# Mixer weights by rows, without a copy at the start, and a shorter last chunk: what each part is worth in a recurrent attention and mixer kernel

## The chip, the cores and the metric

One core of one Trainium2 chip. The metric is device time in microseconds (us) of one execution of the whole program; lower is better. Absolute times differ between chips by up to 16 us for the same kernel, so kernels are compared by their ratio to the kernel before, run on the same chip in the same rounds.

## The reference

Two layers, each an attention over 64 segments of 32 tokens with 8 memory tokens that pass from segment to segment, and a mixer MLP whose four quarters of `h` are shifted by one or two tokens. Cut to what matters:

```python
# x: (1, 2048, 640); 32 heads of 192; w1, w2 640x640; w3 640x1536; w4 1536x640
def _A_ref(x, mem0, Wq, Wk, Wv, Wo, seg_len):
    mem = mem0
    for s in range(n_seg):                       # 64 segments, one after another
        h = concat([mem, x[segment s]])          # 40 tokens
        q, k, v = h @ Wq, h @ Wk, h @ Wv
        o = softmax(mask(q k^T * scale)) v @ Wo
        mem = o[:, :8];  outs.append(o[:, 8:])

def _B_ref(x, w1, w2, w3, w4):
    h = gelu(layernorm(x) @ w1)                  # 640
    g0..g3 = the quarters of h, shifted by +1, -1, +2, -2 tokens
    x1 = x + concat([g0, g1, g2, g3]) @ w2
    return x1 + gelu(layernorm(x1) @ w3) @ w4

x = x + A(layernorm(x));  x = x + B(layernorm(x))     # layer 1
x = x + A(layernorm(x));  x = x + B(layernorm(x))     # layer 2, same weights
```

## The kernel before

The kernel runs the two layers side by side, layer 2 five segments behind layer 1: 69 attention steps, and beside them 35 mixer chunks of 128 columns (two layers of 64 tokens). Chunk c runs beside steps 2c+2 and 2c+3; chunk 33 runs beside the last step, 68, and chunk 34 alone behind it. In layer 1 chunk 34 has nothing, in layer 2 the last 34 tokens.

A planner puts every instruction in order. Each is given a time at which it is due, in units of `STEP` = 48 us. Weights that are not resident pass through a ring of 16 tiles of 128x768. Attention and mixer share the ring; the largest share of each is a constant, and the loads of a share that is full wait in the plan. Attention weights are loaded by the SP queue, mixer weights by GpSimd.

```python
RING = 16          # weight tiles in the ring
RING_A = 14        # at most for attention
RING_B = 6         # at most for the mixer
STEP = 48.0
W3 = (0.7, 0.04)   # w3's n-th product is due at base + STEP * (0.7 + 0.04 n)
W4 = (1.5, 0.025)
W2 = (0.4, 0.04)
...
def load_b(c, nm, n, due):                       # one mixer weight tile
    b = ring("rb")
    k = {"w1": n, "w3": KC + n, "w2": KC + FC - 4 + n}.get(nm)
    if nm == "w4":
        src, rd = w4_v[:, n, :], []
    elif nm == "w2" and n < 4:
        src, rd = B_w2[QD * n:QD * n + P, :], []
    else:
        src, rd = wbd[k], [B("wbd", k)]          # from scratch memory
    ...                                          # nc.gpsimd.dma_start(out=..., in_=src)

def order_mixer_weights():                       # at the start, DRAM to DRAM
    for n in range(KC):                          # w1: column blocks made contiguous
        ... nc.gpsimd.dma_start(out=o, in_=w1[:, :, QD * n:QD * n + P])
    ...                                          # a part of w2, and w3 (12 copies)
    for n in range(FC):
        ... nc.gpsimd.dma_start(out=o, in_=B_w3.rearrange("(kc p) n -> p kc n", p=P)[:, :, P * n:P * n + P])
...
# chunk(c): w1, three output blocks in a PSUM bank, one weight tile per output block
for n in range(a, e):
    wb, wv = load_b(c, "w1", n, due)
    for kc in range(KC):
        nc.tensor.matmul(out=o[:, n - a, :], lhsT=w[:, kc * P:(kc + 1) * P],
                         rhs=vT[:, kc, 4:XB + 4], start=(kc == 0), stop=(kc == KC - 1))
...
# chunk_end(c): w4
for n in range(FC):
    wb, wv = load_b(c, "w4", n, due)             # y2 += h2T[n]^T w4[n], 2 matmuls of 320
...
# the order is final; at most 10 transfers of the SP queue are in flight
for o in placed:
    ins = o.fn(o)
    if o.dma and o.e == "SP":
        if len(flight) >= FLIGHT:                # FLIGHT = 10
            ...                                  # waits for flight[-FLIGHT]
```

## Time and profile before

| | before |
|---|---|
| median of 3 runs | 3567.71 us (3561.39 to 3569.81) |
| span of the profiled run | 3573.5 us |
| first attention step ends | 106.5 us |
| from there to the end of step 67 | 3364.0 us |
| step 68 and chunk 33, to chunk 33's last product | 55.7 us |
| chunk 34 alone, to the end | 47.3 us |

The last four rows are the stages. They come from the view of busy time in chosen stretches. Its columns are start:end, length, then busy us and count of PE (TensorE), PEld (weight loads), DVE, ACT, POOL (GpSimd), then the granted TensorE clock, the DMA engines' busy share, GB/s. For the kernel before:

```profile
0.00:106.50 106.50, 59.43 (x1172) 48.28 (x1172) 21.35 (x91) 19.93 (x49) 29.34 (x55) 1.00 1.00 345
106.50:3470.50 3364.00, 3270.87 (x82106) 3156.11 (x82104) 2308.03 (x6825) 1660.21 (x3466) 875.51 (x1577) 0.99 0.94 309
3470.50:3526.20 55.70, 50.22 (x1297) 43.54 (x1294) 34.85 (x122) 23.11 (x56) 22.19 (x42) 1.00 0.94 310
3526.20:3573.50 47.30, 18.39 (x145) 12.60 (x141) 19.94 (x49) 7.20 (x15) 21.18 (x38) 0.65 0.34 110
```

The reader is to see three limits: transfers in the first row (share 1.00), TensorE in the second and third (3270.87 of 3364.00), and a chain of latencies in the last (TensorE busy 18 of 47 us, DMA share 0.34).

### The profile page before, as it was taken

The page shows a single profiled execution, that of the slowest core. Times are in us where ns is not written, and L with a number is a line of the kernel's source. Part 1 is how long each engine was busy: PE and PEld are TensorE (multiplying, and loading weights), DVE is VectorE, ACT ScalarE, POOL GpSimd, SP SyncE. Part 2 cuts the span into 40 slices and gives each one's busy share as a digit, 9 for nine tenths or more (in the row PEclk, how much of TensorE's full clock was granted, in tenths as well). Part 3 has the DMA queues.
Part 4 walks back from the last instruction along what each step waited for, and adds up shares of the span by engine and source line. Part 5 has one row for each costly group of instructions (what it writes and reads, how often), then busy time and mean ns, then how long its engine had stood idle before and what let it go on. Part 6 is the DMA issues. An engine that isn't in the chain of part 4 may idle for free.

```text
span 3573.5 us, 194593 instructions
## 1 busy us (share of the span) xinstructions
PE 3398.9 (95%) x84703; PEld 3260.5 (91%) x84703; DVE 2384.2 (67%) x7085; ACT 1710.5 (48%) x3584; POOL 948.2 (27%) x1712
## 2 busy tenths in 40 slices
PE   5899999999999999999999999999999999999996
PEld 4788999999999999999999999999999999999885
DVE  2456667777676777776666777776767777776555
ACT  2344555554454555544455555454545555444432
POOL 3022222222222222222222222222222222222224
PEclk9999999999999999999999999999999999999898
DMA  9999999999999999999999999999999999999996
GB/s 342 310 314 312 305 302 304 310 308 308 309 307 313 314 308 304 316 300 308 306 308 311 311 301 305 308 319 308 309 311 310 311 306 313 309 304 316 310 313 207
DMA packets 735993, 1097.76 MB, mean 307 GB/s; under 512 B 97374, under 2 KB 693612, under 8 KB 735136
## 3 DMA queue, kind: packets, MB, share of 16 engines
q1 hardware_dynamic: 669504, 874.19, 74.6%
q0 software_dynamic: 65632, 211.12, 17.9%
q8 instruction: 662, 10.85, 1.3%
q14 instruction: 195, 1.60, 0.1%
HBM read 1079.68 MB, written 8.19 MB: 304 GB/s over the span
## 4 chain that ended last, share of the span: by engine, by line
PE 69%; DMA 19%; issue 9%; POOL 2%; DVE 1%; ACT 0%; POOLq 0%; SPq 0%; ACTq 0%; DVEq 0%
PE psy L669 14%; PE psq L530 12%; PE psv L571 11%; PE psk L530 11%; DMA wst<-in_A_Wk_dram 7%; DMA wst<-in_A_Wq_dram 5%; PE psvt L583 4%; DMA wst<-in_B_w_dram 4%; PE pss L602 3%; PE pso L650 3%; PE psh L993 3%; DMA wst<-in_A_Wv_dram 3%; PE pst L635 2%; PE y L1011 2%; POOL wst L465 1%
## 5 line engine op out<-in xcount | busy, mean ns | idle before, releaser
L530 PEld LDWEIGHTS <-wst 128*128 128x128 bf16 x13248 | 551.9, 100 | 75.1 <-DMA wst<-in_A_Wk_dram 41.3
L587 ACT COPY V<-psvt 80x768 bf16<-80x768 bf16 (+1 forms) x552 | 438.2, 794 | 327.7 <-PE psvt L583 326.2
L465 POOL DMA_DIRECT2D wst<-in_B_w_dram x560 | 303.6, 542 | 1005.2 <-PE psk L530 250.6
L656 DVE CAST oT<-pso 128x480 bf16<-128x480 f32 (+1 forms) x552 | 340.8, 617 | 341.7 <-PE pso L650 341.0
L465 POOL DMA_DIRECT2D wst<-wbd x630 | 339.6, 539 | 724.8 <-PE pss L602 229.5
L669 PE MATMUL psy<-oT,wo 128*128 128x80 bf16 (+1 forms) x10350 | 509.6, 199 | 11.2 <-DMA wo<-in_A_Wo_dram 5.1
L538 ACT CAST qT<-psq 128x480 bf16<-128x480 f32 (+1 forms) x552 | 292.3, 530 | 428.8 <-PE psq L530 427.5
L530 PE MATMUL psk<-hT,wk 128*128 128x80 bf16 (+1 forms) x9936 | 482.7, 199 | 7.9 <-ACT hT L707 4.2
L571 PE MATMUL psv<-hT,wv 128*128 128x80 bf16 (+1 forms) x9936 | 466.6, 199 | 6.5 <-DMA wv<-in_A_Wv_dram 4.3
L530 PE MATMUL psq<-hT,wq 128*128 128x80 bf16 (+1 forms) x9936 | 454.5, 199 | 9.8 <-DMA wq<-in_A_Wq_dram 8.7
L577 ACT CAST vTs<-psv 128x480 bf16<-128x480 f32 (+1 forms) x552 | 292.3, 529 | 337.2 <-PE psv L571 335.5
L669 PEld LDWEIGHTS <-wo 128*128 128x128 bf16 x10350 | 425.6, 100 | 21.3 <-issue 9.2
L530 PEld LDWEIGHTS <-wk 128*128 128x128 bf16 x9936 | 411.6, 99 | 21.9 <-issue 8.8
L571 PEld LDWEIGHTS <-wv 128*128 128x128 bf16 x9936 | 399.8, 100 | 18.7 <-DMA wv<-in_A_Wv_dram 5.7
L613 DVE CUSTOM_DVE_ANT_1 pss<-pss,mask 80x320 f32<-80x320 f32 (+1 forms) x512 | 245.4, 479 | 253.8 <-PE pss L602 252.3
L530 PEld LDWEIGHTS <-wq 128*128 128x128 bf16 x9936 | 395.5, 100 | 16.3 <-DMA wq<-in_A_Wq_dram 9.5
L530 PE MATMUL psk<-hT,wst 128*128 128x80 bf16 (+1 forms) x6624 | 359.0, 199 | 32.2 <-DMA wst<-in_A_Wk_dram 28.2
L571 PE MATMUL psv<-hT,wst 128*128 128x80 bf16 (+1 forms) x6624 | 368.0, 199 | 8.7 <-DMA wst<-in_A_Wv_dram 4.8
L625 DVE TENSOR_REDUCE sm<-pss 80x4 f32<-80x320 f32 (+1 forms) x552 | 252.7, 458 | 153.6 <-ACT pss L620 153.1
L669 PE MATMUL psy<-oT,wst 128*128 128x80 bf16 (+1 forms) x6210 | 353.0, 199 | 1.0 <-DMA wst<-in_A_Wo_dram 0.5
L530 PE MATMUL psq<-hT,wst 128*128 128x80 bf16 (+1 forms) x6624 | 333.2, 200 | 16.3 <-DMA wst<-in_A_Wq_dram 14.3
L546 DVE CAST kT<-psk 128x320 bf16<-128x320 f32 (+1 forms) x552 | 254.7, 461 | 136.9 <-PE psk L530 132.6
(119 smaller groups left out, 5768.8 us busy)
## 6 DMA issues: line engine op xcount, KB each, us to landing
wst<-in_A_Wk_dram SPq DMA_DIRECT2D x1104, 192.0 KB, 4.7
wst<-in_A_Wq_dram SPq DMA_DIRECT2D x1104, 192.0 KB, 4.9
wst<-in_A_Wv_dram SPq DMA_DIRECT2D x1104, 192.0 KB, 4.9
wst<-in_A_Wo_dram SPq DMA_DIRECT2D x1242, 160.0 KB, 4.4
wst<-wbd POOLq DMA_DIRECT2D x630, 160.0 KB, 5.1
wst<-in_B_w_dram POOLq DMA_DIRECT2D x560, 160.0 KB, 4.9
wk<-in_A_Wk_dram SPq DMA_DIRECT2D x8, 576.0 KB, 7.3
wq<-in_A_Wq_dram SPq DMA_DIRECT2D x8, 576.0 KB, 7.5
```

The source lines that it names most:

```text
L465: return (nc.sync if B_SP else nc.gpsimd).dma_start(out=T(b)[:, 0:Dm], in_=src)
L530: nc.tensor.matmul(out=o[:, c, 0:N], lhsT=w[:, c * P:(c + 1) * P], rhs=h[:, kc, c0:c0 + N], start=pq.begin(), stop=True, skip_group_check= ...
L538: nc.scalar.copy(out=q[:, :, 0:N], in_=T(pq)[:, :, 0:N])
L546: nc.vector.tensor_copy(out=k4[:, :, 0::3, 0:N], in_=p4[:, :, 0::2, 0:N])
L571: nc.tensor.matmul(out=o[:, c, 0:N], lhsT=w[:, c * P:(c + 1) * P], rhs=h[:, kc, c0:c0 + N], start=pv.begin(), stop=True, skip_group_check= ...
L577: nc.scalar.copy(out=vs[:, :, 0:N], in_=T(pv)[:, :, 0:N])
L583: nc.tensor.transpose(out=T(pt)[0:N, c, :], in_=vs[:, c, 0:N], identity=ident[:, :])
L587: nc.scalar.copy(out=V_[0:N, :, 0:Dh], in_=T(pt)[0:N].rearrange("n c f -> n (c f)").rearrange("n (i e) -> n i e", i=HG))
L613: nc.vector.tensor_tensor_reduce(out=o, in0=o, in1=maskt.unsqueeze(1).to_broadcast([N, HG, N]), scale=-scale, scalar=3.0e38, op0=ALU.add, ...
L625: nc.vector.reduce_sum(out=sm_[0:N, 4:4 + HG], in_=o, axis=AX.X)
L656: nc.vector.tensor_copy(out=o_[:, :, 0:N], in_=T(pso)[:, :, 0:N])
L669: nc.tensor.matmul(out=T(psy[j])[:, m - m0, c0:c0 + N], lhsT=w[:, m * P:(m + 1) * P], rhs=o_[:, c, 0:N], start=psy[j].begin(), stop=True, ...
```

## The change

The intent: w1 and w3 are read by rows straight from the inputs, so that no rearranged copy is needed; the loops over output blocks and over the inner dimension change places, and two PSUM banks stay open. The last chunk is cut to the 72 columns that it needs, and its input rows and all its weights are loaded early into attention weights that are done with. Chunk 33 is made due earlier. The mixer's share of the ring falls from 6 to 5 slots. Cut to its core:

```diff
-RING_B = 6
+RING_B = 5
-W3 = (0.7, 0.04)
+W3 = (0.75, 0.055)
+W1 = (0.15, 0.04)
 ...
 def load_b(c, nm, n, due):
+    if c == NCH - 1:
+        return ahead[nm, n]
     b = ring("rb")
-    (scratch memory or input)
+    wd, src = mixer_src(nm, n)      # rows of w1, w2, w4; half rows (128x768) of w3
 ...
-def order_mixer_weights(): ...      # 24 copies, 2.95 MB
 ...
+def prefetch(c):                    # the last chunk's 32 weight tiles, on the SP queue
+    for i, (nm, n) in enumerate(units):
+        b, tl = resident["kqv"[i // 3 % 3], i // 9]      # a freed attention weight
+        ... nc.sync.dma_start(out=tl[:, i % 3, 0:wd], in_=src)
 ...
 def chunk(c):
-    D = lambda x: base + x * STEP
+    D = lambda x: base + x * STEP * (0.6 if c == NCH - 2 else 1.0)
+    last = c == NCH - 1
+    xn = XL if last else XB         # 72 or 128 columns
+    if last:
+        prefetch(c)
 ...
-    w1: for n: (load tile n) for kc: matmul
+    pz = [ps("B", [P, 3, XB], f32, "psh") for _ in range(2)]
+    for kc in range(KC):
+        wb, wv = load_b(c, "w1", kc, due)
+        for n in range(KC):
+            nc.tensor.matmul(out=T(pz[n // 3])[:, n % 3, 0:xn], lhsT=w[:, P * n:P * n + P],
+                             rhs=vT[:, kc, 4:xn + 4], start=pz[n // 3].begin(), stop=True, ...)
 ...                                 # w3 likewise, in two halves of 5 tiles
 def chunk_loads(c):
+    if c == NCH - 1:                # rows into a freed tile, not into xo behind its store
+        ... nc.gpsimd.dma_start(out=xl_view()[1:2 * (S - w0):2, :], in_=x2d[w0:S, :])
```

## The prediction

> **What bounds the kernel now.** I read the page's head first, then the busy time in chosen stretches, then the waits of TensorE, then the timelines of the last 50 us. The first two views show three stages with different limits (columns of the stretches: start:end, length, then busy us and count of PE, PEld, DVE, ACT, POOL, then granted clock, DMA share, GB/s):
>
> ```profile
> span 3573.5 us, 194593 instructions
> PE 3398.9 (95%) x84703; PEld 3260.5 (91%) x84703; DVE 2384.2 (67%) x7085; ACT 1710.5 (48%) x3584; POOL 948.2 (27%) x1712
> ...
> 20.00:40.00 20.00, 9.27 (x167) 7.27 (x168) 2.62 (x10) 3.07 (x7) 9.99 (x17) 1.00 1.05 367
> 60.00:80.00 20.00, 14.84 (x295) 11.98 (x292) 5.17 (x22) 5.13 (x12) 0.00 (x0) 1.00 1.07 371
> ...
> 2000.00:3000.00 1000.00, 980.20 (x24359) 955.24 (x24356) 704.95 (x2033) 505.45 (x1033) 265.89 (x478) 1.00 0.95 309
> ...
> 3530.00:3550.00 20.00, 7.64 (x50) 5.39 (x51) 10.42 (x28) 2.68 (x6) 9.64 (x17) 0.50 0.27 84
> ```
>
> The start (to about 107 us, where the first attention step ends) is bound by transfers: 367 to 371 GB/s while TensorE is 46 to 74% busy. The middle is bound by TensorE with transfers close behind: 24,359 matmuls in 1000 us is 41 ns each, and TensorE idles only 20 us of 1000. An attention step takes about 50.5 us there (from the copies that pass the memory tokens on); what I can add up from start to start of its matmuls without gaps over 60 ns is about 48.6 us, so only some 1.8 us a step, 36 us of each 1000, is waiting. The waits say for what (waiter, what ended it, us in all, times, longest):
>
> ```profile
> PE psk L530 <- DMA wst<-in_A_Wk_dram: 28.2, 47, 1.6
> PE y L1011 <- DMA wst<-in_B_w_dram: 16.4, 30, 1.6
> PE psq L530 <- DMA wq<-in_A_Wq_dram: 8.7, 7, 3.5
> ...
> PEld L530 <- DMA wst<-in_A_Wk_dram: 41.3, 77, 1.7
> PEld L1011 <- issue: 22.3, 44, 1.8
> ```
>
> The end is a chain of latencies: TensorE 38% busy at clock 0.50. In the timelines (start, length, operation, and in brackets the idle time before it), the last attention product ends at 3520.35; then come chunk 33's last product and the whole of chunk 34:
>
> ```profile
> 3520.35 2.06 PE L1011 MATMUL y<-wst,h2T 128*128 128x320 bf16 x14
> 3524.02 2.18 PE L1011 MATMUL y<-wst,h2T 128*128 128x320 bf16 x10 [1.61 <-DMA wst<-in_B_w_dram]
> 3537.80 2.83 PE L939 MATMUL psh<-vT,wst 128*128 128x128 bf16 x25 [0.78 <-ACT vT L914]
> 3550.86 5.17 PE L993 MATMUL psh<-vT,wst 128*128 128x128 bf16 x60 [0.83 <-ACT vT L981]
> 3561.34 1.24 PE L1011 MATMUL y<-wst,h2T 128*128 128x320 bf16 x6 [0.85 <-DMA wst<-in_B_w_dram]
> ...
> 3529.52 0.62 POOL L815 MEMSET xo<- 128x640 bf16 x1
> 3530.43 0.58 POOL L823 DMA_DIRECT2D xo<-x2d  x1 [0.29 <-POOL xo L815]
> ...
> 3532.56 0.82 DVE L861 TENSOR_TENSOR xw<-psx,xo 128x640 f32<-128x640 bf16 x1 [2.23 <-DMA xo<-x2d]
> ```
>
> From 3520.35 to the end are 53 us, about 1.5% of the span.
>
> **What the Trainium skill says.** (1) "TensorE: Matmul & The Clock Gate", What's actually happening: the array runs at 1.2 GHz until some 3.4 us of sustained work, and at 2.4 GHz after. The trace agrees: in the tail 25 matmuls of 128 columns took 2.83 us, 113 ns each, beside 128/1.2 = 107; in the middle I read 56.7 ns between starts. So a column saved in the tail is worth twice one in the middle. (2) "DMA: Bandwidth & Descriptors", Issuing engines are not separate DMA queues: transfers from every queue share the same 16 engines. The trace agrees: from 20 to 40 us the two queues' packets add up to a share of 1.05, so the copies take their time from the attention weights. (3) The same page, Why small descriptors are slow (HBM only), puts an overhead of 27% on 256-byte descriptors. The copies' rows are 256 bytes, but their packets show as 2048 to 4096 bytes and took 0.044 ns a byte (share of 16 engines' time not divided out), as the 1536-byte rows of the attention weights do (0.045 to 0.048). I use the measured rate. (4) "PSUM — Partial Sum Buffer", The four PSUM rules: of several groups open in one bank only the first matmul may clear. The new w1 and w3 loops do this; it costs no instruction, and no time in this trace bears on it.
>
> **The change part by part.**
>
> Start. The copies of w1, w3 and a part of w2 into scratch memory go: 16 of 160 KB and 8 of 40 KB, 2.95 MB by the list of transfers. At the 367 GB/s of that stretch they take 2.95/0.367 = 8.0 us of all 16 engines; the packets' own durations give the same 8 us. The stage is at its transfer limit, so this comes off whole: -8 us. The 21 us of GpSimd issuing (3.5 + 4.0 + 3.5 + 10.0) was hidden beneath it and counts for nothing more.
>
> Middle, 33 chunks. Bytes are unchanged: before 34 loads of 160 KB, after 22 of 160 and 10 of 192, both 5440 KB. TensorE's matmuls are the same in number and shape (25, 10, 60, 24), in another order. GpSimd has two loads less of 0.54 us, at 27% busy: hidden. VectorE's last GELU step of w1 goes from 6 pieces to 9, some 0.3 us each, +0.9 us in 101 us at 70% busy: hidden. The mixer may hold 5 ring slots of 16 instead of 6, so attention has 11 at the least instead of 10, which should take a little from the waits on Wk and Wq and may add to those on w4 (y). Against it, w1 and w3 hold two PSUM banks through their whole sum. I can't fix the sign from the profile; I take -4 us in all, 0.1 us a chunk.
>
> Tail, by the instruction order of the changed kernel:
> - Chunk 33 is due earlier: 8 of its 24 last products now stand before the last attention product, 16 behind it. 16 at 147 ns (2.06/14) are 2.4 us, the 8 moved cost 1.2 us earlier, beside 5.75 us now (with the 1.61 us wait): -2.2.
> - Chunk 34 no longer waits for xo to be stored, cleared and reloaded. Now the sum into xw starts 6.4 us after the last y matmul; then only two VectorE additions (0.9 us) stand between: -5.4.
> - w1 on 72 columns: 25 at 72/1.2 = 60 ns are 1.5 us. The first GELU must wait for all 25, where it waited for 15 (1.85 us), so little is won there; its steps on 216 instead of 384 elements save 0.6 us, and the second's likewise: -1.2.
> - The w2 product and the layer norm are the same: 0.
> - w3 and w4 now take 11.7 us (3550.86 to 3562.58), with 1.6 us of waits for w4 that the early loads remove. After: 60 at 60 ns are 3.6; two GELUs of the second half behind the last matmul, 0.35 + 2 x 0.64 + 0.38 + 0.37 = 2.4; the last 6 products at 0.2, 1.2: 7.2. So -4.5, and I keep -4.3.
> - The last store and the 10 us behind it stay.
> Sum -13.1.
>
> All: -8 - 4 - 13 = -25, so 3567.7 - 25 = 3543 us.
>
> **The rivals.** (a) The middle gets worse: with five slots and both PSUM banks held, w4's products wait more. For it: y already waits 16.4 us, and its weight loads 22.3. Against: w3 now asks for a tile only every 2.6 us (0.055 x 48) where it was 1.9. One us more a chunk is +35: 3578. (b) The middle gets better: the waits on streamed Wk and Wq add up to 106 us on matmuls and weight loads together (28.2 + 41.3 + 14.3 + 21.8); a slot more could take a third: 3508. Against: the transfers at 309 GB/s show a share of 0.95, so there is little room to run ahead. (c) The copies were hidden anyway, the start waiting for something else: 3551. Against: the DMA share over 1 at that time, and a chain there that is nearly all weight transfers. (d) The early loads for chunk 34, 5.57 MB, some 16 us at 340 GB/s, come in the way of chunk 33's w4 loads; its products then wait some 5 us: 3548.
>
> **Range and chances.** Start and tail are sums of measured pieces, together -21, give or take 6. The middle is multiplied by 33 chunks, so half a microsecond a chunk is 16 us; it sets the range: 3519 to 3562. A gain over 2% needs a time under 3496, 47 us below my number and possible only if a good third of all waits in the middle goes: 0.04. A loss over 2% (above 3639) would take 2.9 us a chunk against me: 0.01. Within 2%: 0.95.
>
> **What would show it right or wrong.** The first attention step's end moves from 106.6 to about 98 us with the share still over 1 (if it stays, c). Middle steps stay at 50.5 us within 0.3; y's waits for B_w tell (a), Wk's and Wq's tell (b). From the last attention product to the end falls from 53 to about 41 us: xw's sum about 1 us behind the last y of chunk 33, no DMA wait in the last w4 products (else d). The prediction is wrong if the middle moves by more than 20 us either way, or if the compressed chunk 33 makes the last attention step longer than it saves behind it.

## The result, and the profile after

The changed kernel took 3557.69 us (median of 4 runs, 3554.08 to 3563.53) against 3565.85 (4 runs, 3561.39 to 3569.81) of the kernel before in the same rounds: ratio 0.9979, 95% interval 0.9960 to 0.9998. That is within 2%, as predicted, and inside the range (3519 to 3562), but 15 us above the number 3543. A later run of the same kernel on another chip (`again` below) gave 0.9963. The two together are a gain of about 0.3%, 10 us, where 25 were predicted.

The head of the page after:

```profile
span 3561.7 us, 194567 instructions
PE 3393.0 (95%) x84693; PEld 3256.4 (91%) x84693; DVE 2378.8 (67%) x7184; ACT 1710.2 (48%) x3583; POOL 884.5 (25%) x1581
```

Busy time in the same four stages, after:

```profile
0.00:99.80 99.80, 59.95 (x1174) 48.40 (x1175) 21.38 (x91) 20.02 (x49) 10.28 (x30) 1.00 0.99 338
99.80:3468.40 3368.60, 3264.34 (x82103) 3152.31 (x82101) 2307.47 (x6924) 1661.94 (x3465) 851.88 (x1511) 1.00 0.94 308
3468.40:3530.80 62.40, 55.08 (x1298) 45.87 (x1294) 34.80 (x125) 22.78 (x56) 19.39 (x36) 0.86 0.93 307
3530.80:3561.70 30.90, 13.65 (x135) 9.81 (x132) 15.12 (x46) 5.42 (x14) 2.97 (x4) 0.63 0.30 103
```

The lengths say where the time went: start 106.5 to 99.8 (-6.7), middle 3364.0 to 3368.6 (+4.6), last step and chunk 33 55.7 to 62.4 (+6.7), chunk 34 47.3 to 30.9 (-16.4). The first and the last stage gained 23 us, but 7 of these came back in the stage of chunk 33; start and tail together gained 16, where 21 were predicted, and the middle did not give its 4. The middle's own difference cannot be read from two traces: the kernel before, profiled again on another chip, took 3377.1 there.

TensorE's waits after (waiter, what ended the wait, us in all, times, longest):

```profile
PE pst L619 <- DVE Pm L611: 18.8, 31, 0.6
PE y L1044 <- DMA wst<-in_B_w_dram: 16.0, 29, 1.2
PE psv L555 <- DMA wst<-in_A_Wv_dram: 14.8, 21, 2.0
...
PE psk L514 <- DMA wst<-in_A_Wk_dram: 6.6, 13, 1.0
```

The wait that headed the list before, for Wk, fell from 28.2 to 6.6 us, and waits that had been small came up in its place: pst for VectorE (1.7 before, now 18.8), psv for streamed Wv (4.8, now 14.8). The wait of y for mixer weights stayed (16.4, now 16.0). A wait that becomes shorter in this list is therefore no gain by itself; the sum of the middle is what counts. Nor is a wait that comes up a loss by itself: the one of pst turns up, at 17.4 to 18.2 us of the middle, in every kernel by rows with 5 slots, and every one by rows with 6 slots has one of psq for ScalarE instead, 20.2 or 20.3 us (`ring6` below). They come with the order in which the planner puts the instructions.

The timelines of the last 60 us after (start, length, operation, idle time before it in brackets; TensorE first, then VectorE and GpSimd):

```profile
3501.96 0.80 PE L1022 MATMUL psh<-vT,wst 128*128 128x128 bf16 x6 [2.19 <-issue]
...
3525.00 4.01 PE L1044 MATMUL y<-wst,h2T 128*128 128x320 bf16 x12
3529.21 0.43 PE L1044 MATMUL y<-wst,h2T 128*128 128x320 bf16 x2 [0.20 <-DMA wst<-in_B_w_dram]
3530.42 0.43 PE L1044 MATMUL y<-wst,h2T 128*128 128x320 bf16 x2 [0.78 <-DMA wst<-in_B_w_dram]
...
3536.97 1.06 PE L965 MATMUL psh<-vT,wk 128*128 128x72 bf16 x15 [0.78 <-ACT vT L940]
...
3548.85 0.88 PE L1022 MATMUL psh<-vT,wk 128*128 128x72 bf16 x12 [0.83 <-ACT vT L1011]
...
3556.17 0.71 PE L1044 MATMUL y<-wq,h2T 128*72 128x320 bf16 x4
...
3531.73 0.82 DVE L880 TENSOR_TENSOR xw<-psx,wk 128x640 f32<-128x640 bf16 x1
...
3557.95 0.57 POOL L1062 DMA_DIRECT2D out_dram<-xo  x1 [11.36 <-DVE xo L1050]
```

Chunk 34 is as intended. Its sum into xw starts 0.9 us after chunk 33's last product, where it was 6.4 us; the 25 matmuls of w1 have 72 columns (the line shows the first 15); the last products of w4 read resident tiles (`wq`) and wait for no transfer. In chunk 33 the 16 products behind the last attention product are there as predicted, but 12 of them took 4.01 us, 334 ns each, at half clock. TensorE ran at half clock from 3501.3 to 3511.5, where the first line shows it resuming after an "issue" stall of 2.19 us, and again from 3521.8 to 3528.6; the repeat of the kernel has a stall of 1.1 us at that place. Where the stall comes from stays open. The half clock is most of what made this stage longer: the same 1297 or so matmuls kept TensorE busy for 55.1 us instead of 50.2 (granted clock of the stage 0.86 instead of 1.00), and that is 4.9 of the 6.7 us. The rest is waiting.

The last row holds one more thing that nobody had asked about: the program ends with a drain of GpSimd. The view of the closing line's instructions (durations in ns as least/median/most, first and last start) before:

```profile
L1132 POOLq DRAIN  x3: 46/93/9135, 3563.6 to 3573.3; - x3
```

and after:

```profile
L1164 POOLq DRAIN  x3: 46/162/2680, 3557.9 to 3561.5; - x3
```

The longest drain is 9.1 us before and 2.7 us after. The difference is 6.5 of the 16.4 us gained in the last stage, and the prediction had counted them as unchanged.

### The profile page after: what moved, and what is told of

Read it like the earlier page. It is cut to its first block, busy times and chain, and to the rows that moved or that the text cites. A ratio compares the mean times of both kernels' runs of the same rounds, so it can differ in the third digit from the quotient of the medians.

```text
span 3561.7 us, 194567 instructions
## 1 busy us (share of the span) xinstructions
PE 3393.0 (95%) x84693; PEld 3256.4 (91%) x84693; DVE 2378.8 (67%) x7184; ACT 1710.2 (48%) x3583; POOL 884.5 (25%) x1581
## 5 line engine op out<-in xcount | busy, mean ns | idle before, releaser
L472 POOL DMA_DIRECT2D wst<-in_B_w_dram x1088 | 597.1, 549 | 1736.2 <-PE pss L586 284.7
L653 PE MATMUL psy<-oT,wo 128*128 128x80 bf16 (+1 forms) x10350 | 510.4, 199 | 10.6 <-DMA wo<-in_A_Wo_dram 5.1
L514 PE MATMUL psk<-hT,wk 128*128 128x80 bf16 (+1 forms) x9936 | 481.6, 199 | 11.7 <-issue 4.6
L514 PE MATMUL psq<-hT,wq 128*128 128x80 bf16 (+1 forms) x9936 | 474.9, 199 | 13.0 <-DMA wq<-in_A_Wq_dram 9.0
L555 PE MATMUL psv<-hT,wv 128*128 128x80 bf16 (+1 forms) x9936 | 453.7, 199 | 5.2 <-DMA wv<-in_A_Wv_dram 2.7
L653 PEld LDWEIGHTS <-wo 128*128 128x128 bf16 x10350 | 423.8, 99 | 18.8 <-issue 6.8
L514 PEld LDWEIGHTS <-wq 128*128 128x128 bf16 x9936 | 407.5, 99 | 27.8 <-DMA wq<-in_A_Wq_dram 9.9
L555 PEld LDWEIGHTS <-wv 128*128 128x128 bf16 x9936 | 391.2, 100 | 15.2 <-DMA wv<-in_A_Wv_dram 4.1
L555 PE MATMUL psv<-hT,wst 128*128 128x80 bf16 (+1 forms) x6624 | 350.9, 199 | 19.3 <-DMA wst<-in_A_Wv_dram 14.8
L624 ACT COPY PT<-pst 80x320 bf16<-80x320 bf16 (+1 forms) x552 | 222.3, 403 | 288.0 <-PE pst L619 284.8
L653 PE MATMUL psy<-oT,wst 128*128 128x80 bf16 (+1 forms) x6210 | 338.5, 199 | 0.3
L604 ACT ACTIVATE pss<-pss,sm 80x320 f32<-80x320 f32 (+1 forms) x552 | 262.2, 475 | 141.2 <-DVE sm L597 141.1
```

Source lines behind the costliest of these rows:

```text
L472: return (nc.sync if B_SP else nc.gpsimd).dma_start(out=T(b)[:, 0:wd], in_=src)
L514: nc.tensor.matmul(out=o[:, c, 0:N], lhsT=w[:, c * P:(c + 1) * P], rhs=h[:, kc, c0:c0 + N], start=pq.begin(), stop=True, skip_group_check= ...
L555: nc.tensor.matmul(out=o[:, c, 0:N], lhsT=w[:, c * P:(c + 1) * P], rhs=h[:, kc, c0:c0 + N], start=pv.begin(), stop=True, skip_group_check= ...
L604: nc.scalar.activation(out=o, in_=o, func=ACT.Exp, bias=sm_[0:N, 0:1], scale=-1.0)
L624: nc.scalar.copy(out=Pt[0:N, :, 0:N], in_=T(pst)[0:N, :, 0:N])
L653: nc.tensor.matmul(out=T(psy[j])[:, m - m0, c0:c0 + N], lhsT=w[:, m * P:(m + 1) * P], rhs=o_[:, c, 0:N], start=psy[j].begin(), stop=True, ...
```

## The experiments

Sixteen kernels ran, in four calls, each call on one chip together with the kernel before. Each has 6 runs, and the kernel before 11 in each call; the prediction's own pair has 4 each. All outputs are right. Letters in the quoted expectations name theories as they stood before that run: S, that the early due time of chunk 33 packs the last step too tightly; C, that the early loads of chunk 34 take transfer time from chunk 33's w4; and the rest are spelled out where they appear. The table has the stages of each profiled run in us, and beside it the ratio to the kernel before.

| kernel | start | middle | step 68 + chunk 33 (of it to step 68's end) | chunk 34 and end (of it the drain) | ratio, 95% |
|---|---|---|---|---|---|
| before | 106.5 | 3364.0 | 55.7 (50.0) | 47.3 (9.1) | 1 |
| before_again | 106.5 | 3377.1 | 54.8 (49.2) | 46.6 (9.1) | 0.9993 (0.9975-1.0011) |
| the change | 99.8 | 3368.6 | 62.4 (56.7) | 30.9 (2.7) | 0.9979 (0.9960-0.9998) |
| again | 98.5 | 3364.1 | 61.6 (56.3) | 30.9 (2.7) | 0.9963 (0.9943-0.9982) |
| no_squeeze | 99.2 | 3360.6 | 63.8 (52.0) | 30.9 (2.7) | 0.9965 (0.9942-0.9988) |
| no_early_weights | 98.8 | 3372.9 | 60.8 (58.1) | 35.2 (4.8) | 0.9975 (0.9953-0.9998) |
| copies_kept | 105.7 | 3373.4 | 58.9 (52.6) | 38.1 (10.1) | 1.0031 (1.0007-1.0055) |
| copies_plain | 106.5 | 3370.5 | 61.5 (55.4) | 30.8 (3.1) | 0.9995 (0.9974-1.0015) |
| rows_only | 99.0 | 3378.2 | 61.4 (51.2) | 43.6 (4.8) | 1.0017 (0.9999-1.0035) |
| rows_pace | 99.2 | 3391.5 | 63.4 (53.8) | 43.7 (4.8) | 1.0061 (1.0037-1.0085) |
| before_ring5 | 105.9 | 3362.5 | 61.3 (51.0) | 47.5 (9.2) | 1.0015 (0.9995-1.0035) |
| rows_ring6 | 99.2 | 3367.5 | 57.8 (49.3) | 43.8 (4.7) | 0.9992 (0.9970-1.0014) |
| middle_only | 106.1 | 3363.5 | 59.4 (51.4) | 41.8 (3.3) | 0.9996 (0.9973-1.0019) |
| ring6 | 99.5 | 3353.5 | 61.1 (55.4) | 30.4 (2.7) | 0.9955 (0.9933-0.9976) |
| ring6_no_squeeze | 98.9 | 3353.3 | 66.3 (54.2) | 30.4 (2.7) | 0.9942 (0.9922-0.9962) |
| ring6_gentle | 99.9 | 3367.5 | 60.2 (56.5) | 31.0 (2.6) | 0.9945 (0.9926-0.9965) |
| ring6_no_early | 98.8 | 3363.4 | 57.0 (53.3) | 35.6 (4.7) | 0.9942 (0.9926-0.9959) |
| ring7 | 99.5 | 3422.5 | 57.9 (55.6) | 30.4 (2.6) | 1.0085 (1.0065-1.0105) |

How far to trust a cell: the start and the last stage agree to about 1 us wherever the same thing is done. Step 68 and chunk 33 do not: `again`, `copies_kept` and `copies_plain` have the change's order of TensorE there, and these four traces run from 58.9 to 62.4. A difference under some 3.5 us between two cells of that column is not shown by them. Part of it is the granted clock: for nearly the same count of matmuls TensorE was busy 50.2 us at clock 1.00 (before), 52.9 at 0.93 (`before_ring5`), 55.1 at 0.86 (the change) and 56.2 at 0.86 (`ring6_no_squeeze`). No run was made to hold the clock apart from the rest.

The middle scatters more. TensorE's order in `no_squeeze`, `no_early_weights` and `rows_only` is the same as the change's until the last steps, so their middles are repeats of one another, and they run from 3360.6 to 3378.2. A middle is only worth comparing by many runs, or by the ratios.

### First call: undo one part at a time

**no_squeeze**, chunk 33 due as all others:

```diff
-        D = lambda x: base + x * STEP * (0.6 if c == NCH - 2 else 1.0)
+        D = lambda x: base + x * STEP * 1.0
```

> The change with chunk 33 due as before (factor 1.0 instead of 0.6), nothing else; its order on TensorE is that of the change up to the last two attention steps. In the change's trace the last attention step took 56.7 us (before: 50.0) and the last product of chunk 33 ended 62.2 us after the step before it (before: 55.4). Theory S (the earlier due time pulls chunk 33's w3 and w4 into the last attention step, where the ring has no room): last step about 50, chunk 33 ends about 55 after, time 5 to 7 us less than the change, about 3551. Theory C (the early loads for chunk 34 take the transfer time of chunk 33's w4): chunk 33 still ends 60 or more after, the time within 2 us of the change. Theory X (the 2.2 us stall and half clock in the one trace were chance): last step 50 to 52, but the time within 2 us of the change, about 3557.

Measured: 3566.5 us, ratio 0.9965. Step 68 itself ends earlier (52.0 instead of 56.5 us), but 11.8 us of chunk 33 are then left behind it instead of 5.5, and the stage is 63.8 us long. So the early due time is not what made the stage longer: without it the stage is no shorter. S falls. That the early due time gains the 2 us is less than the scatter and not shown.

**no_early_weights**, the last chunk's weights through the ring as they come:

```diff
-        if c == NCH - 1:
-            return ahead[nm, n]
...
-        if last:
-            prefetch(c)
```

> The change with chunk 34's weights loaded through the ring from GpSimd as before, everything else kept (72 columns, its rows early, chunk 33 early). Theory S: last attention step again about 56, chunk 33 ends 61 to 63 us after the step before. Theory C: chunk 33 ends about 57 after, w4 waits of its products (2.4 us in the change) gone. Theory X: last step 50 to 52. For all: chunk 34 waits for w1 and w4 again, some 3 us; and the GpSimd drain at the end, 9.1 us before and 2.7 us with the change, is near 9 again if it is the recent GpSimd loads that it waits for, near 3 if not. Time 3560 to 3567.

Measured: 3569.86 us, ratio 0.9975. The last stage is 35.2 instead of 30.9 us, step 68 and chunk 33 60.8 instead of 62. So the early loads give 4.3 us (2.1 of them in the drain). The waits of chunk 33's w4 products fell from 2.4 to 0.3 us without them, as C has it, but the stage is only 1.2 us shorter, which is inside the scatter.

**copies_kept**, the copies made as before, but never read:

```diff
+    wbd = dram.tile([KC + FC + 1, P, Dm], bf16, name="wbd")
...
+        order_mixer_weights()
```

> The change with the copies of w1, w3 and w2 into scratch memory issued again at the start, read by nobody. If the start is bound by transfers: first attention step ends at 106 to 107 us instead of 99.8, and the time is 6 to 8 us over the change, about 3564.5. If a later stage absorbs the start: first step late as said, the time within 2 us of the change.

Measured: 3586.41 us, ratio 1.0031. The first step ends at 105.7 us again, so the copies cost 6 to 7 us of start and were not hidden. They also bring the long drain back (10.1 us). Start and drain, 14 us together, leave some 8 of the difference to the change unexplained; of the size of the scatter in the middle.

**rows_only**, the rows and the share of 5, none of the parts of the end:

```diff
-        if c == NCH - 1:
-            return ahead[nm, n]
...                                 # rows of the last chunk loaded as all others'
-        (0.6 if c == NCH - 2 else 1.0)
+        1.0
...
-        last = c == NCH - 1
+        last = False
```

> The change without its tail parts: weights by rows and no copies, but chunk 34 on 128 columns, rows and weights loaded as before, chunk 33 due as before. Last attention product to the end again about 53 us (change: 36.6), last step about 50. If the middle lost nothing, as predicted, the time is that of before less the 7 us of the start, 3558 to 3560. If the middle pays for the new order of w1 and w3 and the smaller ring (theory M: some 9 to 16 us over 33 chunks, 0.3 to 0.5 us a chunk), it is 3567 to 3574, no better than before.

Measured: 3582.44 us, ratio 1.0017: no gain, although the start is 7 us shorter and the drain 4 us. Step 68 and chunk 33 take 61.4 us without any part of the change meant for them. What is longer there comes with the rows or with the share of the ring (or, in part, with the granted clock, 0.94 here).

### Second call: rows, ring share, pace, copies

**before_ring5**, the kernel before with one number changed:

```diff
-RING_B = 6
+RING_B = 5
```

> The kernel before with the mixer's share of the ring cut from 6 slots to 5 and nothing else. After the first four runs theory S and C have fallen: chunk 33 ends 61 to 64 us after the step before it in every kernel with weights by rows and no copies, early due or not, early weights or not (before: 55.7), and the middle of these kernels costs some 9 us more than it should by their times. Theory R (the smaller ring share is what costs): this one shows it too, chunk 33 ends 59 or more after, and the time is 8 to 12 us over that of before. Theory O (the order: no GELU until a whole half of w3 has been loaded and multiplied, and its later pace) or theory N (nothing in the middle, noise): time within 4 us of before, chunk 33 at 55 to 57.

Measured: 3579.92 us, ratio 1.0015. Step 68 and chunk 33 take 61.3 us instead of 55.7 and 54.8. TensorE's timeline of chunk 33's end in this kernel:

```profile
3523.69 0.43 PE L1011 MATMUL y<-wst,h2T 128*128 128x320 bf16 x2 [2.91 <-DMA wst<-in_B_w_dram]
...
3528.44 1.22 PE L1011 MATMUL y<-wst,h2T 128*128 128x320 bf16 x4 [0.28 <-DMA wst<-in_B_w_dram]
```

The wait of 2.91 us for a tile of w4 was 1.61 us with 6 slots, and all waits for w4 in the stage were 4.0 us where they were 1.6. The stage is 6 us longer with one slot less, in one trace. Its timeline of GpSimd shows one way to it: 4 of chunk 33's 12 loads of w4, instead of 6, were issued before a clearing for chunk 34 that waits for VectorE, and the other 8 only after it, from 3520.96 us on. But TensorE was also busy 2.7 us longer at the lower clock, so the waits are not the whole of it.

**rows_ring6**, `rows_only` with 6 slots:

```diff
-RING_B = 5
+RING_B = 6
```

> rows_only with 6 ring slots for the mixer instead of 5. Theory R: 8 to 12 us less than rows_only, that is 3 to 7 us below before, and chunk 33 ends at 55 to 57. Theory O or N: within 4 us of rows_only (which was 6 us over before), chunk 33 at about 61.

Measured: 3572.88 us, ratio 0.9992, and 57.8 us in the stage (59.4 in `middle_only` below, which has the same order there). So of the 6 us lost there with rows and 5 slots, 2 to 4 seem to come from the share, which is of the size of the scatter; the rest stays with the rows.

**rows_pace**, `rows_only` with w3 due earlier:

```diff
-W3 = (0.75, 0.055)
+W3 = (0.7, 0.048)
```

> rows_only with w3 due as before (from 0.70 of a step on, the ten tiles over the same 23 us as the twelve before: 0.048 each, instead of 0.75 and 0.055), ring 5. Theory O in the form that the later pace costs: chunk 33 ends 3 to 5 us earlier, 56 to 58, and the time falls some 5 us below rows_only. Theory R or the form of O in which it is the loop order and not the pace: 60 to 62, time as rows_only, 6 us over before.

Measured: 3599.78 us, ratio 1.0061, 0.44% worse than `rows_only`, nearly all in the middle (3391.5). The later, slower pace of w3 that came with the change is needed with 5 slots.

**copies_plain**, the change, and as many bytes copied at the start as the kernel before copies, but in whole rows of 1280 bytes instead of pieces of 256:

```diff
+        for n in range(18):
+            nc.gpsimd.dma_start(out=wbd[n], in_=(w4_v[:, n, :] if n < FC else B_w2[...]))
```

> The change with 18 copies of 160 KB to scratch memory at the start, as many bytes as the removed copies, but each from whole rows: 16 pieces of 10 KB instead of 640 or more of 256 bytes. Tests the GpSimd drain at the very end: 9.1 us before, 10.1 with the copies kept, 2.7 to 4.8 in the three kernels without. If the drain pays for the small pieces of the copies, it is 2.7 here; if for any copy from memory to memory or for the use of scratch memory, about 10. The first attention step ends at 106 to 107 us if its cost is bytes, under 102 if it was the small pieces. Time: 4 to 8 us over the change if the drain is short, 10 to 16 over if it is long.

Measured: 3573.68 us, ratio 0.9995, the first step's end at 106.5 us, as with the small pieces. The cost of the copies is their bytes, not their pieces. GpSimd's time to issue them was longer in the kernel before. Groups of instructions of the kernel before (busy us, mean ns of one, idle before):

```profile
L489 POOL DMA_DIRECT2D wbd<-in_B_w_dram x12 | 10.0, 1306 | 0.6 <-DMA wbd<-in_B_w_dram 0.6
```

and of `copies_plain`:

```profile
L481 POOL DMA_DIRECT2D wbd<-in_B_w_dram x18 | 9.1, 507 | 1.9 <-DMA wbd<-in_B_w_dram 1.3 <-issue 0.4
```

The records last 1306 against 507 ns, but those of the kernel before overlap: 10.0 us busy for 12 copies are 0.83 us each, against 0.51 (not by the pieces alone: its four copies of 32 whole rows took 3.5 us, 0.87 each, as well). Still, the first step ends at the same time: the issuing was hidden, as the prediction had it. The drain is 3.1 us here, so it is not the copying as such that makes it long.

### Third call: the change with 6 slots

**ring6**:

```diff
-RING_B = 5
+RING_B = 6
```

> The change with 6 ring slots for the mixer instead of 5, nothing else. Theory R, which two runs support (6 slots won 9 us on the rows-only kernel, 5 slots cost the kernel before some 5 us and moved chunk 33's end from 55.7 to 61.3 us after the step before): 6 to 10 us less than the change, some 0.9955 of before, chunk 33 ends at 56 to 59 us instead of 62.4. If the gain of rows_ring6 was chance or hangs on the late due time of chunk 33: within 3 us of the change.

**ring6_no_squeeze**, the same with chunk 33 due as all others (the edit of `no_squeeze` besides):

> The change with 6 slots and chunk 33 due as before. With room in the ring, the early due time should pay what the prediction gave it: this one then ends chunk 33 some 2 us later than ring6 and is 0 to 3 us slower. If the early due time is useless with either ring: equal within 2 us, last attention step 49 to 52 here, with chunk 33 at 57 to 58.

**again**, the change unaltered, on the same chip:

> The change itself, unaltered, as the standard for the other three on this chip, and a second trace of it. Expected 0.997 to 0.998 of before, first step 99 to 100 us, drain 2.7. If the 2.2 us stall and the half clock in its last attention step are the rule: last step 55 to 58, chunk 33 at 61 to 63; if chance: 52 to 54, and at 58 to 60.

**middle_only**, `rows_ring6` with the copies back (the edit of `copies_kept` besides): of the whole change only the loops and the source of the weights in the middle are left.

> rows_ring6 with the copies put back (read by nobody): start, drain and ring as in the kernel before, so that only the loops of w1 and w3 over input rows with their due times, and the tiles of w3, differ from it. If these cost nothing in the middle (theory R alone): within 4 us of before, 1.000 to 1.001 with some 2 us at chunk 33. If the order itself costs (theory O, no GELU before a whole half is summed, two PSUM banks held): 6 us or more over before, 1.002.

Measured: ring6 3547.14 us (0.9955), ring6_no_squeeze 3545.2 (0.9942), again 3551.43 (0.9963), middle_only 3561.63 (0.9996). Busy time of the middle and of the next stage in `ring6`:

```profile
99.50:3453.00 3353.50, 3261.79 (x82107) 3152.56 (x82104) 2307.39 (x6924) 1661.35 (x3466) 847.08 (x1511) 0.99 0.94 310
3453.00:3514.10 61.10, 52.31 (x1295) 44.96 (x1292) 35.06 (x125) 22.33 (x56) 18.60 (x35) 0.96 0.93 308
```

`middle_only` shows no cost of the loops by rows in the middle, within the 8 us or so of its interval: with copies and 6 slots the kernel is where it was (0.9996), its shorter drain making good a longer stage of chunk 33. `ring6` has a middle 10.6 us shorter than `again`, beside which it ran, but the medians differ by 4 us only, and the interval of each covers the other. What a slot is worth needs more pairs; they are added up below. In step 68 and chunk 33 the sixth slot gave the full change nothing (61.1), and without the early due time the stage is 66.3.

### Fourth call: is it the early loads, and is more of the ring better?

**ring6_gentle**, early loads of the last chunk with at most 3 in flight instead of 10:

```diff
+            fl = 3 if o in early else FLIGHT
-            if len(flight) >= FLIGHT:
+            if len(flight) >= fl:
```

> ring6 with the early loads for chunk 34 held to 3 in flight instead of 10. Theory C in its narrower form (the early loads slow chunk 33's last w4 loads, whose products waited 2.4 to 5.2 us in the traces with them, 0.3 in the one of the same due time without): the waits of those products fall under 1 us and chunk 33 ends 2 to 4 us earlier than in ring6 (61.1 us after the step before), with no wait for weights in chunk 34; time 2 to 3 us less than ring6, 0.995 of before. If the waits come from how late the loads are issued and not from contention: 61 again. If three in flight are too few: waits of chunk 34's w1 products and a later end.

**ring6_no_early**, `no_early_weights` with 6 slots:

> ring6 with chunk 34's weights through the ring from GpSimd, as in no_early_weights with 6 slots. Theory C: chunk 33 ends at 56 to 58 (61.1 with the early loads), so that they cost 3 to 5 us there and win about 4 behind it: time equal to ring6 within 3 us. If they cost nothing: chunk 33 at 60 to 61, time 3 to 5 us over ring6. The drain shall be 4.8, as in the other kernels with the same list of GpSimd transfers.

**ring7**, the change with 7 slots (`RING_B = 7`):

> The change with 7 slots of the ring for the mixer. The middle (end of the first step to end of the last but one) took 3364 to 3379 us in seven traces of kernels by rows with 5 slots, 3353 to 3368 in four with 6. If it is room for the mixer's weights that the middle lacks: 3345 to 3358, time 0.992 to 0.995 of before. If 6 is the balance: 3358 or more, and no better than ring6.

**before_again**, the kernel before, unaltered, to see the scatter:

> The kernel before, unaltered, for a second trace of it (the first was on another chip) and as a measure of the scatter: ratio 1.000, interval over 1. First step 105 to 107; if the first trace was typical, middle 3362 to 3368, chunk 33 at 55 to 57, drain 9.1. If chunk 33's 55.7 was chance: 58 to 61, and then the ring's share is not what moved it.

Measured: ring6_gentle 3559.26 us (0.9945), ring6_no_early 3556.95 (0.9942), ring7 3609.29 (1.0085), before_again 3576.51 (0.9993).

With 6 slots the early loads cost step 68 and chunk 33 4.1 us (57.0 to 61.1) and give the last stage 5.2 (35.6 to 30.4): next to nothing is left of them. Loading gently gives 0.9 of it back (60.2) and loses 0.6 behind. Both are inside the scatter, and none of these moves the time.

The two parts that meet in chunk 33, put together from single traces (us of step 68 and chunk 33):

| | no early weights | early weights |
|---|---|---|
| 5 slots, due as others | 61.4 (rows_only) | 63.8 (no_squeeze) |
| 5 slots, due early | 60.8 (no_early_weights) | 61.6, 62.4 (again, the change) |
| 6 slots, due as others | 57.8 (rows_ring6) | 66.3 (ring6_no_squeeze) |
| 6 slots, due early | 57.0 (ring6_no_early) | 61.1 (ring6) |

Down each pair of rows: due early gives 0.6 to 0.8 us without early weights and about 2 to 5 with them. Across: early weights cost 1 to 2.5 us with 5 slots and 4 to 8.5 with 6. With a scatter of some 3.5 us, only the cost of early weights with 6 slots and the 5.2 of due early beside them stand out. All cells are above the 55.7 and 54.8 of the kernel before. The two on the right of `due as others` differ by more than the scatter in the unexpected direction (66.3 with the larger share); this was not followed further.

What a slot is worth in the whole kernel, from the ratios of pairs that differ in the share alone: again to ring6 0.9963 to 0.9955; no_squeeze to ring6_no_squeeze 0.9965 to 0.9942; no_early_weights to ring6_no_early 0.9975 to 0.9942; rows_only to rows_ring6 1.0017 to 0.9992. The differences are 0.0008, 0.0023, 0.0033 and 0.0025, on average 0.0022, which is 8 us; before_ring5 against the kernel before, 0.0015, goes the same way. Each by itself is inside the scatter; five of five in one direction is why I hold the sign for settled and the size for rough. Of the four pairs only the first ran on one chip together. The traces agree: the middle is 3361.4 us on average in the six kernels by rows with 6 slots and 3369.8 in the seven with 5 slots and the change's order. What is changed by this one number is not the room alone, though: the planner makes another order of the instructions from it almost from the start, and no run keeps the two apart.

TensorE's waits in `ring6`:

```profile
PE psq L514 <- ACT V L571: 20.2, 29, 0.7
...
PE psk L514 <- DMA wst<-in_A_Wk_dram: 10.2, 25, 1.0
...
PE y L1044 <- DMA wst<-in_B_w_dram: 6.8, 15, 1.1
```

and in `ring7`:

```profile
PE psk L514 <- DMA wst<-in_A_Wk_dram: 29.2, 52, 2.1
PE psv L555 <- DMA wst<-in_A_Wv_dram: 20.1, 40, 1.4
```

The wait of y for w4 is 6.8 us here, where the change has 16.0. With 7 slots for the mixer the attention weights come late (their waits in the middle add up to 73 us, 27 in `ring6`), and the middle takes 3422.5 us; the whole kernel is 0.85% slower than the kernel before. The waits are not all of it: of the 69 us more than in `ring6`, they make 30, and TensorE is busy 34 us longer for the same 82,107 matmuls, which nothing here explains. So the share is a balance, with the best of the three sizes at 6, where the kernel before had it.

**The drain.** Over all 18 traces the longest GpSimd drain at the end is the same to 0.1 us for kernels with the same list of GpSimd transfers: 1314 transfers 2.6 to 2.7 us (7 traces), 1346 transfers 4.7 to 4.8 (5), 1440 transfers 9.1 to 9.2 (3); then 1338 with 10.1, 1332 with 3.1 and 1370 with 3.3, one each. It is not ordered by the number of transfers, by whether copies were made (3.1 and 3.3 with copies), nor by how lately GpSimd had loaded. What sets it stays open.

**A better version.** ring6, ring6_no_squeeze, ring6_gentle and ring6_no_early all lie at 0.9942 to 0.9955, inside each other's intervals. Any of them beats the kernel before by some 20 us (0.55%) and the change as it stands by some 8; ring6, one number changed, is the simplest.

## Why the prediction was right or wrong

- **Start, -8: right.** Measured -6.7, and -8.0 in the repeat (99.8 and 98.5 against 106.5), and two kernels with the copies put back return to 105.7 and 106.5. Rival (c), that the copies were hidden, is refuted; that GpSimd's issuing was hidden is confirmed by `copies_plain`.
- **Middle, -4: wrong, and the largest miss.** What failed is the step that weighed the share of 5 slots: that it "should take a little from the waits on Wk and Wq", from which -4 was made, and only "may add to those on w4 (y)". It did both. In the middle (the list of TensorE's waits, taken for that window alone) the waits for attention weights add up to 22 us after, 41 and 45 in the two traces before. But like compared with like, kernels by rows, y waits for w4 for 0.7 to 3.6 us of the middle with 6 slots (six traces) and 10.9 to 18.8 with 5 (seven traces with the change's order); in the kernel before it goes from 13 and 11 to 26 with 5. The attention weights' waits are some 12 us less with 5 slots, which only balances this; all waits of TensorE together are 101 us on average with 5 and 90 with 6. Most of that net difference stands under "issue", waits for which the profile names nothing (35 against 25 us), so what they wait for stays open. The ratios put the share of 5 at about 8 us of loss. The sum agrees: of the 10 us gained in all, start and end stages account for 6.7 + 16.4 - 6.5, 17 us, which leaves the middle at about +7, not -4 (the two traces of the kernel before are too far apart to show it by themselves).
- **Rivals (a) and (b).** Rival (a) was right in sign and in its cause, five slots. Its mark, longer waits of y, is hidden in the change (16.4 and 16.0 us) because the loops by rows take as much from them: 3.5 us of the middle in `middle_only`, against 13 and 11 before. The two open PSUM banks, its other cause, show no cost within 8 us (`middle_only`). Rival (b) counted waits of matmuls and of their weight loads as 106 us; TensorE's whole idle time in the middle is 93 us (3364.0 - 3270.9), so much of that is counted twice.
- **"Chunk 33 is due earlier": -2.2 predicted, +6.5 measured for its stage.** What failed is the cost of a product and the path beside it: the step took 147 ns for each of 16 products at the end and left the rest of step 68 as it was. 12 of the 16 took 334 ns at half clock, and over the stage TensorE was busy 4.9 us longer for the same matmuls, of 6.7 us in all. The early due time itself may have gained about 2 us (single traces, inside the scatter). The ring share bears on the stage too, taking the kernel before from 55 to 61.3 us; what the early loads add with 5 slots, 1 to 2 us, is not shown. How share, stall and clock hang together stays open.
- **Chunk 34's sum into xw, -5.4: right**, 6.4 to 0.9 us.
- **w1 on 72 columns, -1.2: right to about 1 us.** The time from the start of w1 to that of w3 fell from 13.1 us (12.2 in the repeat) to 11.9.
- **w3 and w4, -4.3: right**, 11.7 to 8.0 us, -3.7. Rival (d), 5 us for the early loads, was right in kind: 1 to 2 us here, inside the scatter, 4 with 6 slots.
- **"The last store and the 10 us behind it stay": wrong, -6.5.** The 10 us were mostly a drain of GpSimd, 9.1 us before and 2.7 after; for the prediction this was luck, as what sets it is not known. I had not looked at what filled them.
- **Range and chances.** The time fell in the range because, as stated, the middle's uncertainty set it. Both large misses, +11 in the middle and +9 at chunk 33, were partly made good by the drain.

The condition that the prediction named for failing at chunk 33, a compressed chunk that makes the last step longer than it saves behind it, looks fulfilled by the numbers (the step is 56.7 instead of 50.0 us), and yet it is not the cause: uncompressed, the stage is longer still.

## What to carry to other kernels

A change that comes with retuned constants has to be taken apart constant by constant: here a ring share changed from 6 to 5 cost about 8 us, nearly as much as the whole change gained. A wait is to be compared between kernels that differ in that constant alone: beside the kernel before, y's wait looked unchanged. When waits on one input fall in the list of waits, look at the length of the stage before counting a gain, because the engine may only wait for something else. And what stands at the end of the program, here a drain, is on the path and belongs in the sum.

## What the Trainium skill lacked or had wrong

- **The drain at the end of a program.** No page has one of this length: GpSimd's closing drain took 2.6 to 10.1 us, all on the path, and was the same to 0.1 us for the same list of GpSimd transfers (15 traces in three groups).
- **"DMA: Bandwidth & Descriptors", Why small descriptors are slow (HBM only).** The page puts an overhead of 27% on 256-byte descriptors and says that joining consecutive ones into packets amortizes this part; it lacks by how much. Here 2.95 MB copied between HBM addresses, most of it in pieces of 256 bytes, show as packets of 2 to 4 KB that took 0.0435 ns a byte, against 0.0413 for the 10 KB packets of `copies_plain` (share of 16 engines' time not divided out), and ended the first step at 105.7 to 106.5 us, against 106.5. On 8 us of copying, 27% would have been about 2 us, an estimate from the page's figure.
- **"DMA: Bandwidth & Descriptors", Anatomy of one DMA — SWDGE (gpsimd) path.** The table calls descriptor generation "small, variable". Here the 24 copies of the kernel before kept GpSimd busy for 21.0 us at the issue, 0.88 each (640 pieces, but also 32 whole rows, 0.87); those of 128 whole rows in `copies_plain` and the loads of 128 rows took 0.51 to 0.55. What makes the difference is not settled here; a number would help where GpSimd is not as idle as it is in this kernel (25% busy).
